# First head pair of a clustered attention kernel: its set-up in a written order, matmuls on zeros instead of warm-up transposes

## The chip, the cores and the metric

The kernel runs on one core of one Trainium2 chip. The metric is the device time of one execution in microseconds (us). The kernel before the change took 858.32 us, the median of three runs (855.65 to 859.44).

## The reference

Three steps. An attention in which a query sees only the keys of its own cluster, then an MLP with SiLU, then a gated MLP.

```python
q_n, k_n, c_n = (normalised q, k, centroids)
q_assign = argmax(einsum('bhsd,hcd->bhsc', q_n, c_n))
k_assign = argmax(einsum('bhsd,hcd->bhsc', k_n, c_n))
mask = q_assign[:, :, :, None] == k_assign[:, :, None, :]
scores = where(mask, scale * q @ k.T, -1e9)
attn = exp(scores - max(scores))
x = (attn / (sum(attn) + 1e-9)) @ v
g = silu(x @ w_in) @ w_out
out = (sigmoid(g @ w_gate) * (g @ w_val)) @ w_out2
```

There are 2 batches, 8 heads, 768 positions, 64 numbers per head and 16 clusters per head. The MLPs work on 1536 tokens of 512 numbers, with hidden sizes 2048 and 1536. All inputs are float32.

## The kernel before, in words

Two heads form a pair, with 64 partitions each, so there are eight pairs. float32 operands are split into a high part, rounded to the matmul's type, and a low part, the rest. For q, the high part is qh and the low part ql; for k, kh and kl.

`load(p)` fetches qq, kk and vv of pair p, 384 KB each (lines 83 to 92). `prep(p)` (line 174) makes a pair ready:

- It casts qh and kh on ACT and subtracts for ql and kl. For pair 0 that is on DVE, for later pairs on POOL. These four buffers are single (pool `st`), so a later pair's casts must wait until everything that reads the earlier pair's has ended.
- Twelve transfers inside the chip, 192 KB each, lay the halves out for the score matmuls (lines 199 to 205), six for each head j: qa holds qh and ql side by side, ka holds kh twice, and the upper or lower half of q2 and k2 (qm, km) holds qh and kl.
- 24 matmuls `pm` multiply the halves with the normalised centroids cc (line 212). DVE sums them into `sim`, and finds the nearest cluster with a maximum, a comparison, a product with `rank`, a second maximum and a last comparison (lines 220 to 243). The result is a one-hot row per position, oh.
- PE transposes oh, and 16 rows per head go into the free half of q2 and k2. For pair 0, ACT and DVE copy them (lines 254 to 264). For later pairs, one ACT copy and four small transfers do it (lines 266 to 273). A score matmul over these rows adds a large negative number wherever the clusters differ.
- ACT and POOL split vv into vs (lines 276 to 279).

Then come the tiles: `scores` (line 288) runs four matmuls into s, DVE takes the row maximum nm, ACT the exponential e. `transposes` turns e into ph and pl on PE, ACT, DVE and POOL. `values` multiplies them with vs. Two tiles of scores run ahead of the rest.

Before pair 0, the centroids are normalised (csq, the r chain, c2), transposed (pc) and split into cc (lines 109 to 140). 13 transposes of the identity run on PE ahead of pc (lines 128 to 130).

The program is written with a framework that reorders instructions by priority and a modelled time, and adds the semaphores. Every engine then runs its own list strictly in order, so an instruction that waits holds up all behind it on that engine. SP issues all DMAs in the order of its list. `issue_after(x)` places DMAs behind the instruction x.

Of the kernel before, what the change touches and what calls it, by code (L numbers as in the profile page):

```python
# [8 lines left out]
F32 = mybir.dt.float32  # L9
# [16 lines left out]
WARM = 13  # L26
# [4 lines left out]
def clustered_attention_then_two_mlps(ctx, tc, qT, kT, v, cen, w1i, w1o, w2g, w2v, w2o, out):  # L31
# [31 lines left out]
    with ExitStack() as att:  # L63
# [29 lines left out]

        cn = cp.tile([P, D], F32, tag="cn", name="cn")
        nc.sync.dma_start(cn, cen)
# [10 lines left out]
        nc.scalar.activation(sq, sq, AF.Sqrt)  # L106

# [15 lines left out]
        nc.vector.reciprocal(r5, r4)  # L123
        c2 = cp.tile([P, 2, D], F32, tag="c2", name="c2")
        nc.vector.tensor_scalar_mul(c2[:, 0, :], cn, r5)
        nc.vector.tensor_scalar_mul(c2[:, 1, :], cn, r5)

        pw = ps_v.tile([P, P], F32, tag="v", name="pw")
        for _ in range(WARM):
            nc.tensor.transpose(pw, ident, ident)  # L130
# [4 lines left out]
        nc.vector.memset(cc.bitcast(F32), 0.0)  # L135
        pcv = pc[:, 0:P].rearrange("p (h j c) -> p h j c", j=2, c=C)
        for j in range(2):
            r = slice(j * D, (j + 1) * D)
            nc.vector.tensor_copy(cc[r, :, j, 0, :], pcv[r, :, j, :])
            nc.vector.tensor_tensor(cc[r, :, j, 1, :], pcv[r, :, j, :], cc[r, :, j, 0, :], op=ALU.subtract)  # L140


        rank = cp.tile([P, 4 * NT, C], BF16, tag="rank", name="rank")
        for c in range(C):
            nc.vector.memset(rank[:, :, c : c + 1], float(C - c))

        rowscale = cp.tile([P, 1], F32, tag="rowscale", name="rowscale")
        nc.vector.memset(rowscale[0:D, :], -MASKED)
        nc.vector.memset(rowscale[D:P, :], 1.0)


        ex = sm.tile([P, 1], F32, tag="ex", name="ex", bufs=1)
        nc.scalar.activation(ex, cc[:, 0, 0, 0, 0:1], AF.Exp)

        q2, k2 = [], []
        for i in range(2):
            for lst, nm in ((q2, "q2"), (k2, "k2")):
                t = cp.tile([P, 2, S], R32, tag=f"{nm}_{i}", name=f"{nm}_{i}")  # L160
                nc.gpsimd.memset(t[D:P, 0].bitcast(F32), 0.0)
                nc.gpsimd.memset(t[0:D, 1].bitcast(F32), 0.0)
                lst.append(t)

        oh = []
        for i in range(2):
            t = cp.tile([P, NT, 4, 32], BF16, tag=f"oh_{i}", name=f"oh_{i}")
            nc.gpsimd.memset(t, 0.0)
            oh.append(t)

        heads = {}
        L, U = slice(0, D), slice(D, P)

        def prep(p):
# [12 lines left out]
            dma = nc.sync.dma_start  # L187

            nc.scalar.activation(qh, qq, AF.Copy, scale=scale)
            if p == 0:  # L190
                nc.vector.scalar_tensor_tensor(ql, qq, scale, qh, op0=ALU.mult, op1=ALU.subtract)
            else:
                nc.gpsimd.tensor_scalar(qq, qq, scale, 1.0, op0=ALU.mult, op1=ALU.mult)
                nc.gpsimd.tensor_tensor(ql, qq, qh, op=ALU.subtract)
            yield
            cast(nc.scalar, kh, kk)
            (nc.vector if p == 0 else nc.gpsimd).tensor_tensor(kl, kk, kh, op=ALU.subtract)
# [9 lines left out]
            for n, (hi, lo) in enumerate(((qh, ql), (kh, kl))):  # L207
                pm = ps_s.tile([P, 512], F32, tag="s", name=f"pm{p}_{n}")
                pv = pm[:, 0 : NT * 4 * C].rearrange("p (t g) -> p t g", t=NT)
                for i in range(NT):  # L210
                    for m, t in enumerate((hi, lo)):
                        nc.tensor.matmul(
                            pv[:, i, :],
                            lhsT=t[:, i * P : (i + 1) * P],
                            rhs=cc[:, p % HP].rearrange("p j a c -> p (j a c)"),
                            start=m == 0,
                            stop=m == 1,
                        )
                yield
                nc.vector.tensor_reduce(  # L220
                    sim[:, n],
                    pm[:, 0 : NT * 4 * C].rearrange("p (t j a c) -> p j t c a", j=2, a=2, c=C),
                    axis=AX.X,
                    op=ALU.add,
                )

            o = oh[p % 2]
            for ns in ((0,), (1,)) if p == 0 else ((0, 1),):
                g, w = 2 * NT * ns[0], 2 * NT * len(ns)
                sg = sim[:, ns[0] : ns[-1] + 1].rearrange("p n j t c -> p (n j t) c")  # L230
                mx = wk.tile([P, w], F32, tag="mx", name=f"mx{p}_{g}")
                nc.vector.tensor_reduce(mx, sg, axis=AX.X, op=ALU.max)
                yield
                eq = wk.tile([P, w, C], BF16, tag="eq", name=f"eq{p}_{g}", bufs=1)
                nc.vector.tensor_tensor(eq, sg, mx.unsqueeze(2).to_broadcast([P, w, C]), op=ALU.is_equal)
                wq = wk.tile([P, w, C], BF16, tag="wq", name=f"wq{p}_{g}", bufs=1)
                nc.vector.tensor_tensor(wq, eq, rank[:, g : g + w], op=ALU.mult)
                yield
# [392 lines left out]
```

## Time and profile before

| | |
|---|---|
| median of three runs | 858.32 us (855.65 to 859.44) |
| the profiled execution, its own time | 857.65 us |
| its span, first to last instruction | 855.6 us |
| PE busy | 812.7 us (95%) |
| DVE, ACT, POOL busy | 544.5, 427.9, 174.5 us |
| DMA, mean over the span | 85 GB/s, 72.46 MB moved |
| first exponential starts | 22.25 us after the span's start |

Times in rows are microseconds from the span's start. In a timeline row, the first number is the start and the second the duration, or, with a count such as x2, the time from the first start to the last end. A bracket at its end gives the engine's idle time before it and what ended that time. "issue" means that the profile names no releaser. In a windows row, each engine has its busy time and its number of instructions; behind POOL stand the granted clock of TensorE, the mean busy share of the 16 DMA engines, and the rate that they moved.

### The profile page before, as it was taken

Reading aid. Unit: us, or ns where it says so; the run is one execution under the profiler, and the core shown is the slowest. Engines: PE = TensorE matmul, PEld = TensorE weight load, DVE = VectorE, ACT = ScalarE, POOL = GpSimd, SP = SyncE. Lnnn points to the kernel's source line nnn. Section 1 sums busy time; section 2 is a strip of 40 time slices with the busy share of each in tenths; the row PEclk is TensorE's granted clock in tenths of the full one; section 3 lists DMA queues with packets and bytes.
Section 4 is the critical chain, followed back from the end, with each engine's and each line's share of the span. In section 5 each row is a group of like instructions: output and inputs, shape, how many; then the busy total and the mean of one; then the engine's idle time right before and its main releaser. Section 6 shows DMA issues by size and latency. Waiting matters only on the chain.

```text
span 855.6 us, 11571 instructions
## 1 busy us (share of the span) xinstructions
PE 812.7 (95%) x4252; PEld 698.9 (82%) x4252; DVE 544.5 (64%) x940; ACT 427.9 (50%) x830; POOL 174.5 (20%) x205
## 2 busy tenths in 40 slices
PE   6898888989989799999999999999999999999998
PEld 5787888978979678888888888888888888888886
DVE  5697697787898886556565556856533656275222
ACT  4686887877969646454154154343334343043200
POOL 5637467466653600000000000000000000000000
PEclk9999999999999999999999999999999999999999
DMA  9552734626540142312212212112111312020012
GB/s 244 145 113 83 177 81 133 171 50 169 122 151 21 47 151 78 113 52 72 74 50 74 71 53 74 53 47 99 50 49 35 115 50 74 25 74 1 0 50 98
DMA packets 25224, 72.46 MB, mean 85 GB/s; under 512 B 4144, under 2 KB 4240, under 8 KB 25168
## 3 DMA queue, kind: packets, MB, share of 16 engines
q1 hardware_dynamic: 25168, 71.73, 28.6%
q8 instruction: 33, 0.54, 0.3%
q14 instruction: 23, 0.19, 0.1%
HBM read 48.27 MB, written 3.19 MB: 60 GB/s over the span
## 4 chain that ended last, share of the span: by engine, by line
PE 75%; DVE 9%; ACT 5%; DMA 5%; issue 3%; SPq 2%; POOL 0%; ACTq 0%; DVEq 0%
PE h L493 15%; PE y L493 15%; PE acc L570 11%; PE ov L493 11%; PE og L493 11%; PE s L290 4%; PE v L339 4%; PE t L320 3%; ACT e L303 2%; DVE nm L298 2%; DVE pl L330 2%; DMA k<-rows 1%; ACT ph L57 1%; DMA kk<-in_kT 1%; DMA qq<-in_qT 1%
## 5 line engine op out<-in xcount | busy, mean ns | idle before, releaser
L57 ACT ACTIVATE wh<-c 128x512 fp32r<-128x512 f32 x68 | 42.8, 632 | 127.6 <-PE y L493 58.9
L320 PE MATMUL t<-ident,e 128*128 128x128 f32 x576 | 89.0, 280 | 9.6 <-DVE pl L330 8.3
L298 DVE TENSOR_REDUCE nm<-s 128x1 f32<-128x768 f32 x96 | 91.1, 949 | 9.1 <-PE s L290 8.2
L330 DVE TENSOR_TENSOR pl<-t,ph 128x384 fp32r<-128x384 f32 x144 | 76.7, 550 | 31.4 <-ACT ph L57 29.2
L303 ACT ACTIVATE e<-s,nm 128x768 f32<-128x768 f32 x96 | 87.0, 907 | 11.6 <-DVE nm L298 10.7
L57 ACT ACTIVATE gh<-g 128x512 fp32r<-128x512 f32 x84 | 53.0, 632 | 76.2 <-DVE g L555 73.7
L505 DVE TENSOR_TENSOR gl<-g,gh 128x512 fp32r<-128x512 f32 x84 | 58.0, 691 | 49.1 <-ACT gh L57 48.8
L339 PE MATMUL v<-ph,vs 128*128 128x256 f32 x288 | 80.7, 307 | 7.3 <-DVE xf L351 5.1
L474 DVE TENSOR_TENSOR wl<-c,wh 128x512 fp32r<-128x512 f32 x68 | 47.7, 705 | 60.5 <-ACT wh L57 60.4
L320 PEld LDWEIGHTS t<-ident,e 128*128 128x128 f32 x576 | 69.2, 143 | 15.7 <-DVE pl L330 10.4
L339 PE MATMUL v<-pl,vs 128*128 128x256 f32 x288 | 79.9, 306 | 1.4 <-DVE pl L330 1.4
L493 PE MATMUL h<-xh,wh 128*128 128x512 f32 x192 | 75.7, 394 | 2.0 <-ACT wh L57 2.0
L493 PE MATMUL h<-xh,wl 128*128 128x512 f32 x192 | 75.4, 393 | 1.3 <-DVE wl L474 1.3
L493 PE MATMUL y<-gh,wh 128*128 128x512 f32 x192 | 74.3, 390 | 1.3 <-issue 1.3
L493 PE MATMUL h<-xl,wh 128*128 128x512 f32 x192 | 75.2, 392 | 0.0
L493 PE MATMUL y<-gh,wl 128*128 128x512 f32 x192 | 74.6, 390 | 0.1
L493 PE MATMUL y<-gl,wh 128*128 128x512 f32 x192 | 74.4, 389 | 0.0
L57 ACT ACTIVATE ph<-t 128x384 fp32r<-128x384 f32 x144 | 67.2, 491 | 13.2 <-PE t L320 12.3
L339 PEld LDWEIGHTS v<-ph,vs 128*128 128x128 f32 x288 | 58.0, 202 | 10.0 <-ACT ph L57 6.1
L290 PE MATMUL s<-ka,qa 128*128 128x384 f32 x192 | 57.3, 381 | 8.5 <-ACT e L303 4.4
L339 PEld LDWEIGHTS v<-pl,vs 128*128 128x128 f32 x288 | 58.2, 202 | 1.6 <-DVE pl L330 1.6
L555 DVE TENSOR_TENSOR g<-ov,g 128x512 f32<-128x512 f32 x36 | 24.9, 692 | 51.8 <-PE ov L493 51.8
(123 smaller groups left out, 1858.9 us busy)
## 6 DMA issues: line engine op xcount, KB each, us to landing
r<-in_w1i SPq DMA_DIRECT2D x16, 512.0 KB, 3.2
r<-in_w1o SPq DMA_DIRECT2D x16, 512.0 KB, 3.2
ka<-kh SPq DMA_DIRECT2D x32, 192.0 KB, 3.9
r<-in_w2g SPq DMA_DIRECT2D x12, 512.0 KB
r<-in_w2v SPq DMA_DIRECT2D x12, 512.0 KB, 3.2
r<-in_w2o SPq DMA_DIRECT2D x12, 512.0 KB, 3.2
qq<-in_qT SPq DMA_DIRECT2D x8, 384.0 KB, 4.8
kk<-in_kT SPq DMA_DIRECT2D x8, 384.0 KB, 3.6
```

The costliest lines, as they stand in the source:

```text
L57: return nc.scalar.activation(o, i, AF.Copy)
L290: nc.tensor.matmul(s[:, g, 0:HS], lhsT=a[:, j, i * P : (i + 1) * P], rhs=c[:, j, g * HS : (g + 1) * HS], start=n == 0, stop=n == 1,)
L298: nc.vector.tensor_reduce(nm, s[:, :, 0:HS], axis=AX.XY, op=ALU.max, negate=True)
L303: nc.scalar.activation(e, s[:, :, 0:HS], AF.Exp, bias=nm, scale=1.0, accum_out=tots[p][:, n : n + 1])
L320: nc.tensor.transpose(t[:, n, :], e[:, kt * P : (kt + 1) * P], ident)
L330: nc.vector.tensor_tensor(lsl, t, hsl, op=ALU.subtract)
L339: nc.tensor.matmul(o, lhsT=vs[:, j, kt, :], rhs=t[:, kt, :], start=kt == 0 and n == 0, stop=kt == NT - 1 and n == 1,)
L474: nc.vector.tensor_tensor(lo, w, hi, op=ALU.subtract)
L493: nc.tensor.matmul(o, lhsT=s[:, k, :], rhs=t[k], start=k == 0 and n == 0, stop=k == KD - 1 and n == 2)
L505: nc.vector.tensor_tensor(gl[k, n], src, gh[k, n], op=ALU.subtract)
L555: nc.vector.tensor_tensor(g, ov, g, op=ALU.mult)
L570: nc.tensor.matmul(o, lhsT=s[k, n][:, sl], rhs=r, start=k == 0 and i == 0, stop=k == KD - 1 and i == 2)
```

## The change

It concerns pair 0 and what is set up before it.

1. Pair 0's preparation leaves `prep` and is written out by hand inside `manual_schedule`, which keeps the written order: the loads cn, qq, kk, the centroids, the casts, the twelve transfers with head 0's six first and vv's load between the two sixes, the clusters and head 0's masks.
2. A mask set now holds q and k of one head (`first_masks(j)`), where it held both heads of q, then of k. Head 0's set is in the written part, head 1's stands in the program behind the first two tiles of scores, as does the split of vv.
3. `load(1)` comes behind the last of the twelve transfers (`issue_after(last.ins)`).
4. The 13 transposes go. In three places, 9, 3 and 10 matmuls of 128x512 on a tile of zeros are issued, the last ten behind pm.
5. Smaller pieces: identb is cast on ACT instead of DVE, cc is built on all 128 partitions in two operations instead of on halves in four (a factor `mine` makes the other head's part zero), `rank` has one row of 16 instead of 24, and the zero fills of q2, k2 and oh are written in another order (`zeros(i)`).

```diff
-WARM = 13
+WARM = (9, 3, 10)
...
+        dma = nc.sync.dma_start
+        first = tc.manual_schedule()
+        first.__enter__()
...
-        load(0)
+        dma(cn, cen)
...
+        dma(qq, qT[0, 0])
+        dma(kk, kT[0, 0])
...
+        wt = cp.tile([P, 512], BF16, tag="wt", name="wt")
+        nc.vector.memset(wt, 0.0)
+        pw = ps_v.tile([P, 512], F32, tag="v", name="pw")
...
+        def warm(n):
+            for _ in range(n):
+                nc.tensor.matmul(pw, lhsT=wt[:, 0:P], rhs=wt, start=True, stop=True)
...
+        warm(WARM[0])
...
-        nc.vector.tensor_copy(identb, ident)
...
+        nc.scalar.activation(identb, ident, AF.Copy)
...
-        for _ in range(WARM):
-            nc.tensor.transpose(pw, ident, ident)
...
+        nc.vector.tensor_copy(cc[:, :, :, 0, :], pcv)
+        nc.vector.tensor_tensor(cc[:, :, :, 1, :], pcv, cc[:, :, :, 0, :], op=ALU.subtract)
+        warm(WARM[1])
...
+        nc.scalar.activation(qh, qq, AF.Copy, scale=scale)
+        nc.vector.scalar_tensor_tensor(ql, qq, scale, qh, op0=ALU.mult, op1=ALU.subtract)
+        cast(nc.scalar, kh, kk)
+        nc.vector.tensor_tensor(kl, kk, kh, op=ALU.subtract)
         for c in range(C):
...
+            nc.vector.memset(rank[:, c : c + 1], float(C - c))
...
+        for j, (r, o) in enumerate(((L, U), (U, L))):
+            dma(qa[r, j].bitcast(F32), qh[r].bitcast(F32))
+            dma(ka[L, j].bitcast(F32), kh[r].bitcast(F32))
+            dma(ka[U, j].bitcast(F32), kh[r].bitcast(F32))
+            dma(qa[o, j].bitcast(F32), ql[r].bitcast(F32))
+            dma(qm[r, j].bitcast(F32), qh[r].bitcast(F32))
+            last = dma(km[r, j].bitcast(F32), kl[r].bitcast(F32))
+            if j == 0:
+                dma(vv, v[0, 0])
...
+        pms = [ps_s.tile([P, 512], F32, tag="s", name=f"pm0_{n}") for n in range(2)]
+        for n, t in enumerate(((qh, ql), (kh, kl))):
+            product_of_clusters(pms[n], 0, t)
+        warm(WARM[2])
...
+        similarities(0, slice(0, 2))
+        similarities(1, slice(0, 1))
+        for _ in first_masks(0):
+            pass
+        first.__exit__(None, None, None)
...
-        for _ in prep(0):
-            pass
         if NPAIR > 1:
-            load(1)
+            with tc.issue_after(last.ins):
+                load(1)
         tiles = [(p, j, i) for p in range(NPAIR) for j in range(2) for i in range(NT)]
         LOOK, LAG = 2, 4
         for t in tiles[:LOOK]:
             scores(*t)
+        zeros(1)
+        for step in (first_masks(1), split_values(vv, vs)):
+            for _ in step:
+                pass
```

The order changes as follows at three places. Names end in numbers: the first is the pair, in s, e and nm the next two are head and tile, in pm, pt, mx, eq, wq and mw the second is a part, and the last number of all is the buffer's.

SP's list, from the first load. Before:

```order
L95 DMA cn_96<-in_cen 128x64
L89 DMA qq0_98<-in_qT 128x768
L90 DMA kk0_99<-in_kT 128x768
L91 DMA vv0_100<-in_v 128x768
L89 DMA qq1_284<-in_qT 128x768
L90 DMA kk1_285<-in_kT 128x768
L91 DMA vv1_286<-in_v 128x768
L200 DMA qa0_192<-qh0_195 64x768
L204 DMA q2_0_176<-qh0_195 64x768
L201 DMA qa0_192<-ql0_196 64x768
```

Now:

```order
L135 DMA qq0_100<-in_qT 128x768
L136 DMA kk0_101<-in_kT 128x768
L232 DMA qa0_173<-qh0_176 64x768
L233 DMA ka0_174<-kh0_178 64x768
L234 DMA ka0_174<-kh0_178 64x768
L235 DMA qa0_173<-ql0_177 64x768
L236 DMA q2_0_127<-qh0_176 64x768
L237 DMA k2_0_129<-kl0_179 64x768
L239 DMA vv0_102<-in_v 128x768
L232 DMA qa0_173<-qh0_176 64x768
```

Head 0's six transfers now stand right behind the first two loads. vv0 comes behind them, and the loads of pair 1 behind all twelve, followed by those of pair 2 as before.

ACT's list, from pair 0's casts to the first exponential. Before:

```order
L57 ACTIVATE kh0_197<-kk0_99 128x768
L57 ACTIVATE vs0_194<-vv0_100 128x6x64 x2
L153 ACT_TABLE_LOAD
L153 ACTIVATE ex_174<-cc_148 128x1
L57 ACTIVATE vs1_336<-vv1_286 128x6x64 x2
L262 ACTIVATE q2_0_176<-pt0_0_262 16x768 x2
L57 ACTIVATE kh1_339<-kk1_285 128x768
L189 ACTIVATE qh1_337<-qq1_284 128x768
L303 ACTIVATE e0_0_0_297,tot0_298<-s0_0_0_290,nm0_0_0_295 128x768
```

Now:

```order
L57 ACTIVATE kh0_178<-kk0_101 128x768
L230 ACT_TABLE_LOAD
L230 ACTIVATE ex_200<-r5_159 128x1
L57 ACTIVATE vs0_175<-vv0_102 128x6x64 x2
L270 ACTIVATE q2_0_127<-pt0_0_264 16x768
L270 ACTIVATE q2_0_127<-pt0_1_315 16x768
L301 ACTIVATE qh1_356<-qq1_275 128x768
L57 ACTIVATE kh1_358<-kk1_276 128x768
L57 ACTIVATE vs1_355<-vv1_277 128x6x64 x2
L370 ACTIVATE e0_0_0_288,tot0_289<-s0_0_0_281,nm0_0_0_286 128x768
```

The casts of pair 1's vv into vs1 stood before pair 0's mask copies, and now stand behind pair 1's other casts and right ahead of the first exponential.

DVE's list, from the end of head 0's mask set to the first row maximum, now:

```order
L256 TENSOR_TENSOR oh_0_131<-wq0_0_258,mw0_0_260 128x6x16 x2
L249 TENSOR_REDUCE sim0_251<-pm0_1_216 128x96
L113 TENSOR_REDUCE mx0_1_305<-sim0_251 128x12
L116 TENSOR_TENSOR eq0_1_307<-sim0_251,mx0_1_305 128x192
L118 TENSOR_TENSOR wq0_1_309<-eq0_1_307,rank_140 128x192
L121 TENSOR_REDUCE mw0_1_311<-wq0_1_309 128x12
L256 TENSOR_TENSOR oh_0_131<-wq0_1_309,mw0_1_311 128x6x16 x2
L271 CAST k2_0_129<-pt0_0_264 16x768
L271 CAST k2_0_129<-pt0_1_315 16x768
L365 TENSOR_REDUCE nm0_0_0_286<-s0_0_0_281 128x1
```

Head 1's whole mask set (mx0_1 to its oh) stands ahead of the copy of head 0's masks into k2. Before, two sets stood there as well, one of q and one of k, with both copies behind them.

## Rows read from the trace of the kernel before

**Rows 1.** The page, parts 1 (busy time of engines) and 4 (chain by engine).

```profile
PE 812.7 (95%) x4252; PEld 698.9 (82%) x4252; DVE 544.5 (64%) x940; ACT 427.9 (50%) x830; POOL 174.5 (20%) x205
...
PE 75%; DVE 9%; ACT 5%; DMA 5%; issue 3%; SPq 2%; POOL 0%; ACTq 0%; DVEq 0%
```

**Rows 2.** Windows of the start: busy by engine, granted clock, DMA share, GB/s.

```profile
2.90:5.20 2.30, 1.47 (x7) 1.47 (x8) 1.82 (x9) 1.10 (x3) 2.14 (x5) 1.00 1.01 375
5.20:12.00 6.80, 5.65 (x28) 5.28 (x26) 3.66 (x10) 3.43 (x6) 5.45 (x7) 1.00 0.99 290
12.00:21.60 9.60, 6.27 (x27) 4.66 (x27) 5.87 (x13) 4.06 (x6) 2.06 (x2) 1.00 1.04 242
...
25.20:34.50 9.30, 9.30 (x74) 9.20 (x72) 5.48 (x9) 5.64 (x13) 4.22 (x5) 1.00 0.88 202
```

**Rows 3.** Timeline, 28 to 37 us: a transfer of pair 1, ACT's longest wait.

```profile
28.55 0.60 SPq L204 DMA_DIRECT2D q<-qh  x1
...
34.56 0.84 ACT L189 ACTIVATE qh<-qq 128x768 fp32r<-128x768 f32 x1 [3.20 <-issue]
```

**Rows 4.** Tile q, the issue at 28.55: time from issue to landing.

```profile
DMA to landing us min/median/max: 5.9/5.9/5.9
```

**Rows 5.** The page, part 6 (DMA issues): count, size of each, time to landing.

```profile
ka<-kh SPq DMA_DIRECT2D x32, 192.0 KB, 3.9
...
qq<-in_qT SPq DMA_DIRECT2D x8, 384.0 KB, 4.8
```

**Rows 6.** Timeline, 0 to 8 us: load, centroids, identity, casts.

```profile
1.18 0.42 SPq L89 DMA_DIRECT2D qq<-in_qT  x1
...
2.60 0.26 ACT L111 ACTIVATE csq<-cn 128x64 f32<-128x64 f32 x1 [0.37 <-DMA cn<-in_cen]
...
3.38 0.29 POOL masks.py:199 TENSOR_SCALAR_AFFINE_SELECT ident<-ident 128x128 f32<-128x128 f32 x1
...
3.73 3.04 PE L130 MATMUL pw<-ident 128*128 128x128 f32 x13 [3.73 <-POOL ident masks.py:199]
...
4.24 0.84 ACT L189 ACTIVATE qh<-qq 128x768 fp32r<-128x768 f32 x1 [1.06 <-DMA qq<-in_qT]
...
4.86 0.35 DVE L126 TENSOR_SCALAR c<-cn,r 128x64 f32<-128x64 f32 x1
...
5.12 0.96 DVE L191 SCALAR_TENSOR_TENSOR ql<-qq,qh 128x768 fp32r<-128x768 f32 x1
...
6.56 0.42 PE L132 MATMUL pc<-ident,c 128*128 128x128 f32 x1
```

**Rows 7.** Timeline, 8 to 23 us: clusters, masks, first scores and exponential.

```profile
8.34 0.40 PE L212 MATMUL pm<-cc,ql 128*128 128x64 f32 x1
...
8.55 0.40 PE L212 MATMUL pm<-cc,qh 128*128 128x64 f32 x1
...
11.84 0.94 ACT L57 ACTIVATE vs<-vv 128x384 fp32r<-128x384 f32 x2 [1.77 <-DMA vv<-in_v]
...
13.57 0.55 DVE L220 TENSOR_REDUCE sim<-pm 128x192 f32<-128x384 f32 x1
...
15.62 0.36 DVE L243 TENSOR_TENSOR oh<-wq,mw 128x192 bf16<-128x192 bf16 x1
...
15.68 0.98 PE L290 MATMUL s<-ka,qa 128*128 128x384 f32 x2 [2.24 <-DVE mw L240]
...
19.19 1.93 DVE L264 CAST k<-pt 16x768 fp32r<-16x768 bf16 x2 [3.22 <-PE pt L254]
...
20.24 1.62 PE L290 MATMUL s<-k,q 128*128 128x384 f32 x4 [1.09 <-issue]
...
22.25 0.90 ACT L303 ACTIVATE e<-s,nm 128x768 f32<-128x768 f32 x1 [0.75 <-DVE nm L298]
```

**Rows 8.** Timeline, 30 to 31 us: two of pair 1's pm matmuls.

```profile
30.49 0.28 PE L212 MATMUL pm<-cc,qh 128*128 128x64 f32 x1
...
30.60 0.28 PE L212 MATMUL pm<-cc,ql 128*128 128x64 f32 x1
```

More of the change, by code (lines that the diff above doesn't have):

```diff
@@ L152, in clustered_attention_then_two_mlps @@
         ex = sm.tile([P, 1], F32, tag="ex", name="ex", bufs=1)
[L153 to L169, printed above, removed]
@@ new lines, in first_masks @@
+        def first_masks(j):
+            sg = sim[:, j].rearrange("p n t c -> p (n t) c")
+            wq, mw = yield from ranked(0, j, sg, 2 * NT)
+            for n in range(2):
+                sl = slice(n * NT, (n + 1) * NT)
+                nc.vector.tensor_tensor(
+                    oh[0][:, :, j, n, 0:C],
+                    wq[:, sl, :],
+                    mw[:, sl].unsqueeze(2).to_broadcast([P, NT, C]),
+                    op=(ALU.not_equal, ALU.is_equal)[n],
+                )
+            pt = ps_t.tile([P, 1024], BF16, tag="t", name=f"pt0_{j}")
+            for i in range(NT):
+                nc.tensor.transpose(
+                    pt[0:D, i * P : (i + 1) * P], oh[0][:, i, j].rearrange("p n c -> p (n c)"), identb
+                )
+            if j == 0:
+                similarities(1, slice(1, 2))
+            r = (slice(D, D + C), slice(0, C))[j]
+            nc.scalar.activation(qm[r, j], pt[0:C, 0:S], AF.Copy, scale=-MASKED)
+            nc.vector.tensor_copy(km[r, j], pt[32 : 32 + C, 0:S])
+            yield
@@ L174, in prep, with split_values @@
+        similarities(0, slice(0, 2))
[3 more added lines that the diff above has]
+        first.__exit__(None, None, None)
+        def split_values(vv, vs):
+            for j in range(2):
+                hi, lo = (vs[:, j, :, L], vs[:, j, :, U]) if j == 0 else (vs[:, j, :, U], vs[:, j, :, L])
+                cast(nc.scalar, hi, vv[:, j])
+                nc.gpsimd.tensor_tensor(lo, vv[:, j], hi, op=ALU.subtract)
+                yield
         def prep(p):
@@ L206, in prep @@
             yield
-            for n, (hi, lo) in enumerate(((qh, ql), (kh, kl))):
+            for n, halves in enumerate(((qh, ql), (kh, kl))):
                 pm = ps_s.tile([P, 512], F32, tag="s", name=f"pm{p}_{n}")
[L209 to L218, printed above, removed]
+                product_of_clusters(pm, p, halves)
                 yield
@@ L274, in prep @@
[L274 to L279 removed]
+            for n in range(2):
+                sl = slice(n * 2 * NT, (n + 1) * 2 * NT)
+                nc.vector.tensor_tensor(
+                    o[:, :, :, n, 0:C].rearrange("p t j c -> p j t c"),
+                    wq[:, sl, :].rearrange("p (j t) c -> p j t c", j=2),
+                    mw[:, sl].rearrange("p (j t) -> p j t", j=2).unsqueeze(3).to_broadcast([P, 2, NT, C]),
+                    op=(ALU.not_equal, ALU.is_equal)[n],
+                )
@@ new lines, in prep @@
+            yield
+            pt = ps_t.tile([P, 1024], BF16, tag="t", name=f"pt{p}")
+            for i in range(NT):
+                nc.tensor.transpose(pt[:, i * P : (i + 1) * P], o[:, i].rearrange("p j n c -> p (j n c)"), identb)
+            rows = wk.tile([P, S], F32, tag="rb", name=f"rows{p}")
+            nc.scalar.activation(rows, pt[:, 0:S], AF.Copy, scale=rowscale)
+            for n, t in enumerate((qm, km)):
+                dma(t[D : D + C, 0].bitcast(F32), rows[32 * n : 32 * n + C])
+                masked[p] = dma(t[0:C, 1].bitcast(F32), rows[64 + 32 * n : 64 + 32 * n + C])
@@ L281, in clustered_attention_then_two_mlps @@
+            yield
+            yield from split_values(vv, vs)
         prob = {}
```

139 lines of the change are left out of this document (65 added, 74 removed).

## The prediction

> **What bounds the kernel now.** I read the page's shares and chain first, then the stages up to 34.5 us, then ACT's longest wait there and the transfer that ends it, then the rows of the start.
>
> Over the whole span PE is the bound: busy 95%, and 75% of the chain that ended last [rows 1]. The change touches only what comes before the first pair runs freely. From the second pair's tiles on, the instructions stand in the same order as before, so whatever the first stage wins or loses goes on to the end one for one, unless something later in that stage waits anyway.
>
> Something does. From 2.9 us the DMA engines are full: shares of 1.01, 0.99 and 1.04, and 0.88 in a last stretch in which the queue runs dry [rows 2]. ACT is idle for 3.20 us, from 31.36, before it casts the third pair's qq into qh at 34.56 [rows 3]. The page names no releaser ("issue"), so I looked for one. The qh buffer is single, so the cast must wait until the second pair's transfers out of it have landed. The last of these is q<-qh, issued at 28.55 and landed 5.9 later [rows 3, 4], at 34.45, 0.11 before the cast. All of ACT's later work stands behind it. I call this **the gate**: PE, DVE and ACT reach it early and wait for the DMA queue.
>
> **The change, part by part, against the gate.** What must land before it is the same in both kernels: nine loads of 384 KB, 23 on-chip transfers of 192 KB (twelve of the first pair, eleven of the second) and the small cn [rows 5]. Only their order and the idle time between them change. I count from the second load's landing; the first is in when qh starts at 4.24 [rows 6]. Prices: 393 kB at 375 GB/s, 1.05 us for a load, and 197 kB at 242 GB/s, 0.81 us for an on-chip transfer [rows 2]. So the second load is in at 5.3.
>
> *The loads' order.* Before, vv0 and the second pair's three loads were queued at once and filled the engines while ACT and DVE made qh, kh, ql and kl. Now the queue runs dry at 5.3. The first transfer needs qh. On ACT the identb cast now stands in front of csq and waits for ident (3.38+0.29=3.67 [rows 6]). Its own 0.3 for 128 columns is an estimate between csq's 0.26 for 64 and qh's 0.84 for 768 [rows 6]. So csq goes from 2.60 to 3.97, and qh from 4.24 to about 4.6, done 5.45. An issue into an empty queue moves data 2.0 later (qq: issued 1.18, in by 4.24, less 1.05 of moving [rows 6]), at 7.45: **2.15 idle**. Three transfers then last to 9.9. The fourth needs ql, which DVE now makes behind cc instead of before it. The scaled centroids were done at 4.86+0.35=5.21, 2.61 after csq began; from 3.97 that is 6.6, so pc stands where it stood, at 6.56. Two cc operations of some 0.35 each (estimated from the c row) and a subtraction of 0.96 [rows 6] behind pc's end at 6.98 give ql at 8.7, and its data at 10.7: **0.8 idle** more. Idle in all: 2.95.
>
> *The gate's new time.* 5.3 + 2.95 + 7 loads x 1.05 + 23 x 0.81 = 34.2 if every transfer has its clean price. Before, the same transfers took from 5.3 to 34.45, 29.15 instead of 26.0; with that duration the gate is at 37.4. The truth lies between, since six loads now stand in one block (clean price) and the on-chip transfers mix as before. I take the middle, 35.8: **+1.35 us**, ends -0.25 and +2.95.
>
> A rule weighed here: the Trainium skill, DMA: Bandwidth & Descriptors, Rules for kernel authors, says to issue a DMA early, compute, and wait late, so that the fixed cost overlaps. It speaks against moving vv0 and the second pair's loads back; by it the sum is +2.95, without it -0.25. The full queue of rows 2 bears it out for the old order.
>
> *Matmuls on zeros for transposes.* The page grants TensorE 1.00 from the start, but the pace says otherwise: pm matmuls start 0.21 apart at 8.34 and 0.11 apart at 30.49 [rows 7, 8]. So the set-up ran at the 1.2 GHz level, after 3.04 us of transposes [rows 6], and later at 2.4. Twenty-two matmuls of 512 columns are added. No row has one at the lower level: four of 384 columns took 1.62 at 20.24 [rows 7], 0.40 each, which bounds one from below; scaled by columns it is 0.54, which bounds it from above, since the 1.62 holds a tail. I take 0.45. Nine (4.1) lie under the loads and are done before pc. Three after pc end near 8.4, and pm began near 8.1 and now waits for ql anyway. Ten stand after pm and *in front of the first scores*: 4.5 at the lower level, half at the upper.
>
> *Masks.* DVE's set for k took 13.57 to 15.98, 2.4 [rows 7]. Now a set holds q and k of one head, but the second head's set still stands on DVE ahead of the first head's k copy, and its transposes on PE ahead of the first mask matmul. So the first exponentials still come two sets, two copies (1.93) and 1.13 (21.12 to 22.25 [rows 7]) after pm's end: 7.9. At the lower level pm ends at 13.6, as before (24 x 0.21 behind 8.5), the ten zeros at 18.1, scores and transposes 3.5 later (15.68 to 19.19) at 21.6, the second copy (0.97) and 1.13 more: 23.7. At the upper, pm's last twelve follow kl (9.7) at 0.11, end at 11.0, and e0 can start at 18.9. The sixteen small memsets of rank move behind kl and lie under pm.
>
> *ACT's order.* e0 now stands behind qh1, kh1 and two vs1 casts (0.94 [rows 7]; they ran at 11.84 before). vv1 lands at 5.3+2.95+12x0.81+4x1.05=22.2, so e0 starts at 23.1 at the earliest, against 22.25, whatever PE's clock. Before, ACT needed 31.36-22.25=9.1 from e0 to the gate; now it arrives at 32.2 to 32.8. The gate is at 35.8, so this loss and any gain on PE are hidden; without that cover the loss would be 0.9 to 1.5. POOL's memsets are the same in number and cost nothing under the loads.
>
> **The sum.** 857.65 (the profiled execution; span 855.6; the median 858.32 is 0.67 higher) + 1.35 = 859.0. Two DVE orders behind the gate differ by an operation; I give them nothing. Half a per cent, 4.3 us, is about what a measurement of this kernel can tell from no change. My forecast is no change.
>
> **Rivals.**
> - *The clock decides, faster.* If zeros lift the clock early and the second pair's loads arrive in time, e0 comes at 18.9, 3.3 earlier, and the four mask matmuls at 20.24 (1.62 [rows 7]) take half, 0.8 less: 853.5. For it: the two paces. Against it: vv1 would have to land at 18, and the gate to come at 30.4, with 26 us of transfers behind 5.3. The Trainium skill, TensorE: Matmul & The Clock Gate, Part 4, says that a transposing matmul does not count as busy for the clock in the same way; by that rule the old warm-up bought nothing and this rival gets its first half. The pace at 8.34 agrees.
> - *The queue starves, slower.* With the bubbles in full, loads at the mixed rate of 290 GB/s (1.36) and transfers at the last stretch's 202 (0.97 [rows 2]), the gate is at 5.3+2.95+9.5+22.3=40.1, 5.6 later: 863.3. It decides once a transfer costs over 0.9. For it: that stretch's rate. Against it: part of that stretch is the queue's own end.
> - *It doesn't do what it says.* The scheduler has put the second head's masks ahead of the first head's scores; if transfers also keep the engines full, both gate and e0 stay: 857.7.
>
> **How the numbers follow.** Forecast 0.62, faster rival 0.13, starved queue 0.13, nothing moved 0.12. The forecast and the last lie within 0.5%: same 0.74. The forecast alone spans 857.4 to 860.6; with half of each outer rival, and the scatter of the three runs (855.65 to 859.44), the range is 854.8 to 862.8.
>
> **What would show it.** Right: a DMA share clearly under 1 between 5.3 and 10.7; ACT's wait before the third pair's qh still there, ended by a landing near 35.8 though PE runs at the faster pace; e0 right behind the vs1 casts at 23 or later. Wrong: no such wait, or a landing by 33 or after 38; e0 before 22; or a difference that appears only behind 60 us, where both orders are equal.

## The result and the profile after

The changed kernel takes 862.31 us, the median of seven runs (861.32 to 866.51); the kernel before, run beside it, 858.32 (855.10 to 860.83). The ratio is 1.0055, 95% interval [1.0028, 1.0082]: slower, by half a per cent. Twelve more runs of the changed kernel gave 1.0038 [1.002, 1.0057]. All 19 have a mean of 862.5, the 42 of the kernel before beside them 859.1: about 3.4 us lost, where the sum had 1.35 and the forecast was no change. The time lies inside the range of the prediction and outside the forecast's own span of 857.4 to 860.6.

The profiled execution took 862.31, its span 860.4. Page, part 1 (busy time of engines) and part 4 (chain by engine), to set against [rows 1]:

```profile
PE 820.5 (95%) x4261; PEld 701.2 (81%) x4261; DVE 545.8 (63%) x943; ACT 427.3 (50%) x831; POOL 174.6 (20%) x205
...
PE 75%; DVE 10%; ACT 5%; DMA 5%; issue 2%; SPq 1%; POOL 1%; POOLq 0%; ACTq 0%; DVEq 0%
```

The bound is the same. Now the start. Windows of the changed kernel, columns as in [rows 2], and then two of the same windows of the kernel before:

```profile
2.90:5.30 2.40, 1.93 (x6) 0.55 (x4) 1.25 (x10) 1.48 (x5) 2.25 (x5) 1.00 0.73 287
5.30:7.50 2.20, 1.06 (x5) 0.49 (x5) 1.61 (x6) 2.17 (x3) 2.20 (x4) 1.00 0.49 113
7.50:10.70 3.20, 2.69 (x13) 2.58 (x14) 1.70 (x18) 0.16 (x1) 1.03 (x2) 0.54 0.94 207
10.70:21.60 10.90, 9.95 (x43) 6.10 (x42) 7.80 (x17) 3.27 (x5) 1.98 (x3) 0.67 1.01 268
```

```profile
2.90:5.30 2.40, 1.57 (x8) 1.57 (x9) 1.92 (x9) 1.13 (x4) 2.24 (x5) 1.00 1.02 376
5.30:7.50 2.20, 1.68 (x8) 1.28 (x6) 2.09 (x5) 0.81 (x1) 2.11 (x4) 1.00 0.88 257
```

The DMA queue, full before, is now short of full by 0.27 x 2.40 + 0.51 x 2.20 + 0.06 x 3.20 = 1.96 us; the kernel before lost 0.26 in the second of these windows. The prediction had 2.95 of idle time.

Timeline of the changed kernel: zeros, pm, the first exponential, and the gate. It answers [rows 3], [rows 6] and [rows 7].

```profile
1.18 3.65 PE L145 MATMUL pw<-wt 128*128 128x512 bf16 x9 [1.18 <-DVE sq L154]
...
6.42 0.81 PE L145 MATMUL pw<-wt 128*128 128x512 bf16 x3
...
8.40 0.40 PE L102 MATMUL pm<-cc,qh 128*128 128x64 f32 x1
8.61 0.40 PE L102 MATMUL pm<-cc,ql 128*128 128x64 f32 x1
...
13.09 4.47 PE L145 MATMUL pw<-wt 128*128 128x512 bf16 x10
...
20.55 0.97 PE L357 MATMUL s<-k,q 128*128 128x384 f32 x4 [0.69 <-DVE k L271]
...
23.36 0.94 ACT L57 ACTIVATE vs<-vv 128x384 fp32r<-128x384 f32 x2 [0.55 <-DMA vv<-in_v]
24.20 0.88 ACT L370 ACTIVATE e<-s,nm 128x768 f32<-128x768 f32 x1
...
29.46 0.46 SPq L313 DMA_DIRECT2D q<-qh  x1
...
36.75 0.84 ACT L301 ACTIVATE qh<-qq 128x768 fp32r<-128x768 f32 x1 [3.77 <-PE pm L102]
```

ACT's wait is still there. Its end, the third pair's qh cast, is what I call the cast below: 36.75 instead of 34.56. The row names pm as releaser, but the second pair's q<-qh lands at 36.60, 0.15 before, and pm had ended long ago. The first exponential stands right behind the vs1 casts, which waited for their load.

The rest of the loss is elsewhere: from the start of the last exponential to the first matmul of the MLP the changed kernel takes 8.14 us, the kernel before 7.54. I call this **the junction**. Timeline there, the kernel before and then the changed one:

```profile
271.26 0.33 SPq L380 DMA_DIRECT2D d_rb<-rt  x1
...
272.62 1.24 SPq L382 DMA_DIRECT2D rb<-d_rb  x2
...
276.63 1.84 POOL L369 TENSOR_TENSOR xf<-xf,rb 128x768 f32<-128x768 f32 x1 [2.62 <-DMA rb<-d_rb]
...
282.34 0.93 ACT L303 ACTIVATE e<-s,nm 128x768 f32<-128x768 f32 x1
...
289.88 0.50 PE L493 MATMUL h<-xh,wh 128*128 128x512 f32 x1 [1.12 <-ACT wh L57]
```

```profile
274.64 0.33 SPq L447 DMA_DIRECT2D d_rb<-rt  x1
...
277.09 1.12 SPq L449 DMA_DIRECT2D rb<-d_rb  x2
...
281.07 1.84 POOL L436 TENSOR_TENSOR xf<-xf,rb 128x768 f32<-128x768 f32 x1 [3.65 <-DMA rb<-d_rb]
...
285.70 0.93 ACT L370 ACTIVATE e<-s,nm 128x768 f32<-128x768 f32 x1
...
293.84 0.50 PE L563 MATMUL h<-xh,wh 128*128 128x512 f32 x1 [1.12 <-ACT wh L57]
```

The seventh pair's row sums go to device memory in a small transfer (d_rb, 6 KB) and come back as rb. SP waits for the first to land before it issues the second: 1.36 between the issues before, 2.45 now, though the order on every engine is the same here (all lists are equal from about 62 us on). POOL starts xf 5.37 after d_rb before, 6.43 now, and behind xf on POOL stand casts that the last `values` on PE wait for. DMA view of the first 1.3 us of this transfer, the kernel before and then the changed one (packets by queue):

```profile
DMA packets 24, 0.01 MB, mean 5 GB/s; under 512 B 12, under 2 KB 24, under 8 KB 24
## 3 DMA queue, kind: packets, MB, share of 16 engines
q1 hardware_dynamic: 24, 0.01, 2.5%
```

```profile
DMA packets 24, 0.03 MB, mean 22 GB/s; under 512 B 11, under 2 KB 22, under 8 KB 22
## 3 DMA queue, kind: packets, MB, share of 16 engines
q8 instruction: 1, 0.02, 5.7%
q14 instruction: 1, 0.01, 2.1%
q1 hardware_dynamic: 22, 0.01, 1.8%
```

The transfer consists of 24 packets. Before, all were through. Now 22 are, and two packets of kind "instruction" have started: program code being fetched. The two are not alike. The one of q8 starts 1.23 behind the issue of d_rb, and the kernel before has one at 1.29, just outside its view, which held nothing. The one of q14 is new at this place: it starts at 1.04 and takes 0.46, where before it started at 5.47. The two packets that are missing from the view move at 1.49 and 1.52, as q14's ends; before, the last moved at 0.95. So the trace points to q14's. The held packets account for 0.57 of the 1.09; the rest of it stays open. What brings such a packet there was a question for the experiments.

### The profile page after: what moved, and what is told of

Its sections match the earlier page's. It is cut to its first block, busy times and chain, and to the rows that moved or that the text cites. A ratio compares the mean times of both kernels' runs of the same rounds, so it can differ in the third digit from the quotient of the medians.

```text
span 860.4 us, 11592 instructions
## 1 busy us (share of the span) xinstructions
PE 820.5 (95%) x4261; PEld 701.2 (81%) x4261; DVE 545.8 (63%) x943; ACT 427.3 (50%) x831; POOL 174.6 (20%) x205
## 4 chain that ended last, share of the span: by engine, by line
PE 75%; DVE 10%; ACT 5%; DMA 5%; issue 2%; SPq 1%; POOL 1%; POOLq 0%; ACTq 0%; DVEq 0%
PE y L563 15%; PE h L563 14%; PE acc L640 11%; PE ov L563 11%; PE og L563 11%; PE v L406 4%; PE s L357 4%; PE t L387 3%; ACT e L370 2%; DVE nm L365 2%; DVE pl L397 2%; ACT ph L57 1%; DMA qq<-in_qT 1%; DMA kk<-in_kT 1%; DVE oh L330 1%
## 5 line engine op out<-in xcount | busy, mean ns | idle before, releaser
L406 PE MATMUL v<-ph,vs 128*128 128x256 f32 x288 | 83.2, 314 | 5.7 <-DVE xf L418 4.1
L406 PE MATMUL v<-pl,vs 128*128 128x256 f32 x288 | 81.7, 311 | 0.0
```

Source lines behind the costliest of these rows:

```text
L406: nc.tensor.matmul(o, lhsT=vs[:, j, kt, :], rhs=t[:, kt, :], start=kt == 0 and n == 0, stop=kt == NT - 1 and n == 1,)
```

## Experiments

All ratios are to the kernel before, run beside on the same chip. "Wait" is the time between the issues of d_rb and rb of the seventh pair.

**The loads' order.** The changed kernel once more, for scatter and for a second profile:

> The changed kernel once more, for a second profile beside the same runs. Queue theory: the first exponential again at 23.5 to 25, the wait before the third pair's qh again ended near 36.6, 861 to 864. Clock theory: if the half-clock stretches fall at other places than in the first profile, the time moves with their number, by up to 1.7 for each; if they fall at the same places, they belong to the program.

Measured: 1.0038 [1.002, 1.0057]; cast 36.20, wait 2.56, junction 8.35.

Loads back in front, in the plainest way:

```diff
+        dma(vv, v[0, 0])
+        load(1)
...
-            if j == 0:
-                dma(vv, v[0, 0])
...
-            with tc.issue_after(last.ins):
-                load(1)
```

> The changed kernel with one part undone: vv0 and the second pair's three loads are issued again right behind the first two, all else as changed (first head's set-up, zeros). Queue theory (the place of the loads costs the time): no idle queue between 5.3 and 7.6 us, ACT's wait before the third pair's qh ends at 34 to 35 instead of 36.6, the first exponential at 21 to 22.5, and the time goes back to 857 to 859.5. Clock theory (the loss is half-clock stretches that the new start brings about at the pair boundaries): time stays at 861 to 864 and the profile has as many half-clock stretches as the changed kernel's. Zeros theory (the ten matmuls in front of the first scores cost it): stays at 861 or more.

Measured: 1.0026 [1.0008, 1.0045], cast 36.50. No clean test: with its data there earlier, the scheduler put vs1 and kh1 in front of the mask copies on ACT, and the first exponential came at 26.38. Only the second pair's loads moved back, in the kernel before (ACT's casts of vs1 and some of POOL's work moved back with them):

```diff
-            load(1)
+            with tc.issue_after(twelve[0].ins):
+                load(1)
```

> The kernel before with one part of the change alone: the second pair's three loads are issued behind the twelve transfers of the first pair (vv0 stays in front). Queue theory: first exponential at 23 to 24.5, the gate 1 to 2.5 later than 34.4, time 860 to 862.5. Clock theory: no change beyond scatter, 857 to 860. Zeros theory: no change, 857 to 860.

Measured: 1.0018 [0.9998, 1.0038], cast 37.72. Against the first profile of the kernel before the gate moved by 3.16; of it 1.0 us (by medians; 1.6 by means) came out at the end, not clear of nothing. So I ran the loads in front with ACT's list held:

```diff
+            with tc.issue_after(copied[0].ins) if p == 1 else nullcontext():
+                nc.scalar.activation(qh, qq, AF.Copy, scale=scale)
```

(and the same for kh1 and vs1; `copied[0]` is the second mask copy).

> The changed kernel with vv0 and the second pair's three loads back in front of the twelve transfers, and ACT's list held as in the changed kernel (the second pair's casts behind the mask copies). Everything else of the change stays. Gate theory (what the change costs is the late loads, through the landing that the third pair's qh cast waits for): that cast is back at 34 to 35.2, from 36.2 and 36.75 in the two profiles of the changed kernel, and the time falls by 1.5 to 2.5, to 860 or below. Theory that the loss lies elsewhere (in what the rest of the change does to the pairs behind): the gate falls as well, and the time stays at 861.5 to 863.

Measured: 1.0028 [1.001, 1.0047], cast 35.25. In this profile the exponentials from the thirteenth to the seventy-ninth start within 1.4 us of the kernel before, on either side (the seventy-ninth 0.11 earlier); the loss comes behind them: 2.3 us in the seventh pair, and a junction of 8.88. The start was undone, and the time only in part.

**The gate, larger and smaller.** Six transfers more in front of it (written to a scratch place, read by nobody):

```diff
+            with tc.issue_after(twelve[0].ins):
+                for n in range(6):
+                    spare = dr.tile([P, S], F32, tag=f"spare{n}", name=f"spare{n}", bufs=1)
+                    nc.sync.dma_start(spare, qT[0, 0])
```

> The kernel before with six more transfers of 384 KB that nobody reads (from the input to a scratch place in device memory), queued behind the first pair's twelve, in front of the third pair's loads and the second pair's transfers. Gate theory, one for one: six times 1.05 to 1.36 put the third pair's qh cast 6.3 to 8.2 later, at 41 to 43, and the time rises by as much, to 864.5 to 867. Theory that the time behind absorbs part of a late gate (as the kernel before with only the second pair's loads moved suggests: cast 3.16 later, median 0.95 higher): a third, 861 to 862.5.

Measured: 1.0068 [1.0043, 1.0093], 5.6 us by medians; cast 40.17, 5.61 later, less than the 6.3 to 8.2 expected. In the time that is one for one, but the scheduler also changed the lists of PE, DVE and ACT up to about 70 us, so the gate is not the only difference. And two transfers less, in the kernel before, where no other engine's list changes:

```diff
+                with tc.issue_after(twelve[0].ins) if p == 2 else nullcontext():
+                    nc.sync.dma_start(kk, kT[b, hp])
+                    loaded[:] = [nc.sync.dma_start(vv, v[b, hp])]
```

> The kernel before with two of the third pair's loads (kk and vv) behind the second pair's twelve transfers instead of in front of them; no other engine's list changes. Gate theory: the third pair's qh cast comes two loads earlier, 2.1 to 2.7, at 31.9 to 32.5, and the time falls by 1 to 2.5. If the first stage is bound by ACT or TensorE as soon as the gate moves forward, or the third pair's kk and vv become late: 0 to 0.5 faster, or slower.

> The kernel before with kk and vv of the third pair behind the second pair's twelve transfers, once more. Gate theory: 1 to 2 under the kernel before, as in the first run (0.998); the cast at 32.5 to 33.5. If the first run was scatter: within 0.5 of it on either side.

Timeline of the first of the two:

```profile
28.12 0.64 SPq L205 DMA_DIRECT2D q<-qh  x1
...
29.79 0.89 SPq L91 DMA_DIRECT2D kk<-in_kT  x1
30.72 0.93 SPq L92 DMA_DIRECT2D vv<-in_v  x1
...
32.64 0.85 ACT L190 ACTIVATE qh<-qq 128x768 fp32r<-128x768 f32 x1 [0.54 <-PE pm L213]
```

Measured: 0.998 [0.9963, 0.9997] and 0.9988 [0.9968, 1.0008]; casts 32.64 and 32.83. The wait of 3.20 has shrunk to 0.54, and both runs come out 1.1 to 1.4 us below the kernel before. The first is the only run whose interval lies below 1. The same edit of the changed kernel:

> The changed kernel with kk and vv of the third pair behind the second pair's twelve transfers; no other engine's list changes. Gate theory: the third pair's qh cast falls from 36.2 to 36.8 to 34 to 35 and the median by 1.3 to 2.2, to 1 to 2 above the kernel before. Theory that the pairs behind lose the time: cast as above, median still 3 above.

Measured: 1.0018 [0.9994, 1.0042], cast 33.70: by the medians about half of the loss is back.

> The version with the loads in front and 13 matmuls on zeros, and with kk and vv of the third pair behind the second pair's twelve transfers. Gate theory: cast at 32.5 to 33.3 and 1 to 2 under the kernel before, about as fast as the kernel before with the same edit (0.998 of it). If ACT is the bound by then (it reaches the cast at 31.4 to 32.8): no more than 0.5 to 1 under.

Measured: 1.0011 [0.9986, 1.0037], cast 34.17, wait 2.42, junction 8.32. No gain: without the two loads moved this version has 0.9994 (below). ACT was idle for only 0.60 ahead of the cast, so the queue hardly holds it any more.

**The gate removed** by a second buffer for qh (`bufs=1 + (t == "qh")`):

> The changed kernel with two buffers for qh instead of one, so that the third pair's cast no longer waits for the second pair's transfers. Gate theory: ACT's wait of 3.5 to 3.9 before that cast goes, and the time falls by 2 or more, to within 1 us of the same edit of the kernel before. Theory that the loss lies elsewhere: the wait goes too, but the time stays 2.5 to 4 above the same edit of the kernel before. If the wait was hidden by later waits in both, neither falls by more than 1.

> The kernel before with two buffers for qh. Gate theory: ACT's wait of 3.20 at 31.36 goes, and 1.5 to 3 of it reach the end: 856 to 857.5. Theory that later waits (on transfers of the second pair, or on the clock's low stretches) take up what the gate gives: 858 to 859.5, no change.

Measured: 1.0038 [1.0018, 1.0057] and 1.0047 [1.0025, 1.0068]. Both expectations of a gain missed. The scheduler moved the cast forward and changed the order behind it as well. In the kernel before the cast now stands ahead of the first exponential and waits 6.46 for the DMA queue, so that the exponential starts at 29.38 instead of 22.25. In the changed kernel the wait is gone and the thirteenth exponential starts at 55.57 (57.61 with one buffer, 55.57 in the kernel before), but the time is no better, with a junction of 8.92 and another order in the pairs. As tests of the gate the two are spoiled by that order; the runs with two loads moved are the clean ones.

**Zeros.**

> The changed kernel without any of the 22 matmuls on zeros (the tile of zeros stays). Queue theory: the zeros lie beside the loads, so the gate stays at 36 to 37 and the time at 861 to 864. Clock theory: TensorE stays at half pace to about 26, the stretches fall elsewhere, time changes by 1 to 3 either way. Zeros theory: 857 to 859.

Measured with `WARM = (0, 0, 0)`: 1.0022 [1.0002, 1.0042], cast 35.49. Its wait is 1.34, but its junction 8.13 (here rb is held: an instruction packet of q8 lies in its time). The interval overlaps those of the changed kernel: the 22 matmuls on zeros gain nothing that shows. (Without them the scheduler also orders the first pair's work otherwise.)

**The fetch of code.**

> The changed kernel with 13 matmuls on zeros (4, 3 and 6) instead of 22, so that TensorE's list has as many matmuls as before; the order behind them stays. Code theory (TensorE's instruction stream is fetched by the same DMA engines in packets, and nine matmuls more have moved a packet onto the two transfers d<-rt and rb<-d of the seventh pair): the wait between these two issues, 2.45 and 2.56 in the profiles of the changed kernel and 1.35 in those of the kernel before, is 1.35 again; the time from the last exponential to the first matmul of the MLP, 8.14 and 8.35, is 7.5 to 7.7; the median is 0.6 to 0.9 under the changed kernel's, so 2 to 3 above the kernel before. Theory that the delay belongs to another part of the change: 2.3 or more, 8.1 to 8.9, no gain. The third pair's qh cast stays at 35.5 to 36.8 by both.

Measured with `WARM = (4, 3, 6)`: 1.0035 [1.0016, 1.0054], cast 35.97, wait 2.57, junction 8.40. Missed: with as many matmuls as before, the delay stays, and the packet of q14 still starts 1.05 behind d_rb. (The order did not stay quite: qh1 and kh1 moved ahead of the second mask copy, and the first exponential came at 26.15.)

> Both suspected costs undone: the loads in front of the twelve transfers with ACT's list held (as in the run before), and 13 matmuls on zeros (3, 0 and 10). If the late gate and the fetch of code are the whole loss: cast of the third pair's qh at 34.5 to 35.3, wait between the two issues of the seventh pair 1.35, last exponential to first MLP matmul 7.5 to 7.7, and the median within 1 of the kernel before. If a third cost is left in the pairs between: 1.5 to 2.5 above it.

Measured, with the loads in front, ACT's list held and `WARM = (3, 0, 10)`: 0.9994 [0.9974, 1.0014], cast 34.89. The loss doesn't show here, though the wait is still 2.40 and the junction 8.30. The same version with two loads moved came at 1.0011 (above), so part of this may be chance.

> The kernel before with nine more small transposes (16 columns) behind the 13, so that TensorE's list has as many matmuls as the changed kernel's; the loads stay as they were. Code theory: the wait between the two issues of the seventh pair rises from 1.35 to 2.3 or more, the time from the last exponential to the first MLP matmul from 7.5 to 8.1 or more, and the median by 0.6 to 0.9. Theory that the delay belongs to another part of the change: 1.35 and 7.5, no change. The third pair's qh cast stays at 34.2 to 34.8.

Measured: 1.0022 [0.9994, 1.0049], wait 2.46, junction 8.54. The delay came as expected, but the nine transposes took 2.13 us and held up pc, and the cast fell to 37.24. So the same with nine matmuls of 16 columns while PE is idle:

```diff
+        for _ in range(9):
+            nc.tensor.matmul(pw[:, 0:16], lhsT=wt[:, 0:P], rhs=wt[:, 0:16], start=True, stop=True)
```

> The kernel before with nine small matmuls on zeros (16 columns) ahead of its 13 transposes, while TensorE has nothing else to do; the order of all else stays. Code theory: the gate stays at 34.2 to 34.8, and the wait between the two issues of the seventh pair rises from 1.35 to 2.3 or more, the time from the last exponential to the MLP from 7.54 to 8.1 or more, the median by 0.5 to 1. Theory that another part of the change makes this delay: 1.35 and 7.5 to 7.6, no change.

Timeline at the junction and DMA view of the transfer's first 1.3 us:

```profile
273.87 0.32 SPq L384 DMA_DIRECT2D d_rb<-rt  x1
...
276.77 1.12 SPq L386 DMA_DIRECT2D rb<-d_rb  x2
...
280.92 1.83 POOL L373 TENSOR_TENSOR xf<-xf,rb 128x768 f32<-128x768 f32 x1 [4.30 <-DMA rb<-d_rb]
...
284.95 0.93 ACT L307 ACTIVATE e<-s,nm 128x768 f32<-128x768 f32 x1
...
293.65 0.50 PE L497 MATMUL h<-xh,wh 128*128 128x512 f32 x1 [1.12 <-ACT wh L57]
```

```profile
DMA packets 23, 0.02 MB, mean 17 GB/s; under 512 B 11, under 2 KB 22, under 8 KB 22
## 3 DMA queue, kind: packets, MB, share of 16 engines
q8 instruction: 1, 0.02, 6.3%
q1 hardware_dynamic: 22, 0.01, 2.3%
```

Measured: cast 34.02, wait 2.90, junction 8.70 instead of 7.54, with nine idle matmuls and the one fill of their tile on DVE as the only edit, 270 us earlier. Again 22 of 24 packets, but beside a packet of q8: it starts 0.35 behind d_rb instead of 1.29 and takes 1.32, and the two late packets move as it ends, at 1.65 and 1.72. So a packet of either queue can hold the transfer, and instructions added at the start can bring it there. In the changed kernel, though, it is q14's that does so. The junction's cost is shown in the trace; in the time, 1.0015 [0.9988, 1.0041], it can't be told from nothing.

> The changed kernel with 20 small matmuls on zeros (16 columns) in front of its first nine; the order of all else stays. Code theory: 40 instructions more move the packet some 4 us ahead of the seventh pair's transfers, the wait between the two issues is 1.35, the time from the last exponential to the MLP 7.5 to 7.7, and the median 0.5 to 1 under the changed kernel's, 2.2 to 3 above the kernel before. Else: 2.3 or more, 8.1 or more, no gain. The gate stays at 36 to 37.

Measured: 1.0055 [1.0028, 1.0081], cast 37.32, wait 2.45, junction 8.21. Missed, and the DMA view of this run says why:

```profile
DMA packets 23, 0.01 MB, mean 10 GB/s; under 512 B 11, under 2 KB 22, under 8 KB 22
## 3 DMA queue, kind: packets, MB, share of 16 engines
q1 hardware_dynamic: 22, 0.01, 1.8%
q14 instruction: 1, 0.01, 1.7%
```

The packet of q8 had moved ahead, as wanted. The one of q14 was still there, and one is enough. The delay isn't due to TensorE's instructions, then: DVE has three more in the changed kernel and ACT one [rows 1]. No run tries which engine q14 serves, but the traces point to DVE. When this packet starts, DVE has begun 448 instructions (waits counted) in all eight profiles with the 940 of the kernel before, and 445 or 446 in ten of the eleven of the changed kernel and its versions, while ACT's count goes from 569 to 593 in the same profiles.

This run also tests the clock rival:

```profile
8.42 0.28 PE L103 MATMUL pm<-cc,ql 128*128 128x64 f32 x1
...
10.65 0.28 PE L103 MATMUL pm<-cc,kl 128*128 128x64 f32 x1
```

Here all pm matmuls run at the faster pace, 0.11 apart, and the last starts at 10.65 instead of 12.88. The first exponential still comes at 24.42, against 24.20.

**Scatter.**

> The kernel before, unchanged. Its median lies within 0.2% of the kernel before run beside it. In its profile the third pair's qh cast starts at 34.2 to 35, the wait between the two issues of the seventh pair is 1.35 and the time from the last exponential to the MLP 7.5 to 7.6; if these differ from the first profile, they are no property of the kernel. The six pairs between take 203.8 in the first profile; 2 more or less would show that their share of the difference is scatter.

Measured: 0.9985 [0.9964, 1.0006]; wait 1.36, junction 7.77; but the cast at 36.10, 1.54 later than in the first profile of the same kernel, with the first exponential at 24.31. The pairs between (thirteenth to eighty-fifth exponential) took 204.3 us, 203.8 in the first profile; over all profiles with one buffer for qh they range from 201.0 to 209.0, the changed kernel's two being 205.1 and 205.7. The expectations above name a clock theory: stretches at the 1.2 GHz level in the pairs. From 40 us to the last exponential the mean granted clock is 0.95 and 0.98 in the two profiles of the changed kernel, with spans of 860.4 and 860.1, and 0.96 and 0.99 in the two of the kernel before, with 855.6 and 858.5. It differs as much between two executions of one kernel, and does not go with the time, so nothing here bears that theory out.

## Why the prediction was wrong

**What held.** The first stage is bound by the queue, and the gate decides: the wait before the third pair's qh cast is there in both kernels, a gate 5.61 later costs 5.6 (with other lists changed too), and one 1.7 to 1.9 earlier than in the first profile gives 1.1 to 1.4 back, with no other list changed. The late loads leave the queue idle between 5.3 and 7.5. e0 stands behind the vs1 casts at 24.20 (I had said 23 or later), so the mask matmuls, now 0.97 instead of 1.62, bring nothing. The rule on early issue, cited from the Trainium skill in the prediction, is borne out at the gate: with the second pair's loads alone moved back, the cast came at 37.72. It has another side: kk and vv of the third pair, moved back behind transfers that were needed sooner, gained.

**The gate's size** was near. With the old loads and order the cast came at 34.56, 34.02 and 36.10 (kernel before twice, and with the small matmuls), with the change's at 36.75, 36.20, 37.32 and 35.97: means of 34.9 and 36.6, 1.7 later, where I had 1.35 (1.5 with the 35.49 of the run without zeros). That it came so near is partly luck, since single profiles of one kernel differ by 1.5, and its parts were off against each other: the idle time is 1.96 instead of 2.95, since DVE had ql done at 8.1 instead of 8.7 and the second bubble hardly exists; and the transfers moved slower than their clean price, about 1.0 us apart instead of 0.81.

**The step that failed** is the sum, which ends at the gate with 1.35 where 3.4 were lost: "whatever the first stage wins or loses goes on to the end one for one, unless something later in that stage waits anyway". I let the change end at the gate, because behind it the instructions stand in the same order, and put all that follows at nothing; a difference that appears only behind 60 us I had named as a sign of being wrong, and there is one. (The lists do differ up to about 62 us, but from the cast to the thirteenth exponential the changed kernel takes 20.86 and 21.33 us, the kernel before 21.01 and 21.57, so that this costs nothing.) From there on the order is the same, but the count of instructions ahead of it is not, and with it the place at which code is fetched. In the changed kernel a fetch falls on a small transfer on which the junction hangs. Junctions: 7.51 to 7.84 in seven profiles of the kernel before and of versions of it without added PE instructions, 8.13 to 8.92 in the eleven of the changed kernel and its versions; 0.6 for the kernel itself (8.14 against 7.54; second profiles 8.35 against 7.77). That a fetched packet holds this transfer is shown by the packets' times in four profiles, and that instructions added at the start can bring it there by the run with nine idle matmuls. Which of the change's instructions moved q14's packet is not shown; the number of matmuls on PE is not the cause, since the delay stays when it is the same as before. The Trainium skill (Runtime: NRT & Kernel Launch, Instruction fetch mechanics) calls the cost of fetching the next block of code mostly hidden; here it is not, in one place: 1.1 us on the transfer, 0.6 at the junction.

**What stays open.** 1.5 to 1.7 at the gate, if it goes on one for one (with only the second pair's loads late, 1.0 to 1.6 of 3.16 did), and 0.6 at the junction are 2.1 to 2.3 of the 3.4. The rest, about 1 us, lies in the pairs between, where single executions of one kernel differ by more than that (204.0 and 202.4 with two loads late); I could not show that it belongs to the change. The traces have a candidate that no run tests. The second pair's row sums take the same way to memory and back, in the kernel before and then the changed one:

```profile
106.10 0.32 SPq L380 DMA_DIRECT2D d_rb<-rt  x1
...
107.44 1.11 SPq L382 DMA_DIRECT2D rb<-d_rb  x2
```

```profile
106.30 0.32 SPq L447 DMA_DIRECT2D d_rb<-rt  x1
...
108.17 1.11 SPq L449 DMA_DIRECT2D rb<-d_rb  x2
```

The issues are 1.34 and 1.87 apart (1.53 and 1.86 in the second profiles), and a packet of q14 starts 0.47 behind the first instead of 4.17. From there to the first exponential of the fourth pair the changed kernel takes 20.23 and 19.88, the kernel before 18.75 and 20.01. It is 19.9 to 21.8 in all eleven profiles of the changed kernel and its versions, and 18.7 to 18.9 in six of the other nine. Whether any of it reaches the end is not shown.

The two versions with the loads in front and ACT's list held differ as well (1.0028 with 22 matmuls on zeros, 0.9994 with 13), and their traces don't tell why. With the loads and nine of the zeros undone the loss no longer shows; which share each has is not settled beyond the gate.

**The clock rival** was wrong for the reason named, that loads set e0: in the run with 20 small matmuls more, pm ran at the faster pace throughout, and e0 came no earlier. Zeros do lift the granted clock, to the 2.4 GHz level from 4.33 on in the first profile (three take 0.81 at 6.42, nine took 3.65), but it was back at 1.2 GHz from 7.74 to 17.98, so that pm ran at 0.21 per matmul as before [rows 7] and the last ten zeros took 4.47. In the second profile of the same kernel it rose at 5.85 and fell at 9.27, and the first pm matmuls started 0.11 apart. It rises behind transposes too: in the kernel before with nine more of them, all pm matmuls start 0.11 apart from 10.05 on, and in the one with six transfers more, behind the usual 13, the first 13 do so from 8.68 on (there too e0 came no earlier, at 22.36). So the sentence on transposes that the prediction cites from the Trainium skill is not borne out by these two profiles; the pace at 8.34 agreed with it in that execution. **The starved queue**, which I gave 863.3, named a price per transfer near the 1.0 us seen, but its gate of 40.1 did not come.

## What to carry to other kernels

Find the transfer that the first stage's longest wait hangs on, and count what is queued in front of it: here two loads that nobody needed yet, put behind it, gave 1.1 to 1.4 us, and were the only edit with a run clearly faster than the kernel before. A small transfer to memory and back with engines waiting on it can be held by code that is fetched on its DMA engines, so a change at the start can cost time at a place that it doesn't touch. Forecast such a change from several profiles if they can be had: one trace gave the gate 1.5 us earlier than another of the same kernel.

## What the runs showed of the hardware

- Code is fetched in packets on the same 16 DMA engines as data (in the changed kernel's page 34 on q8 and 23 on q14, in the kernel before's 33 and 23). One packet beside a 6 KB transfer held two of its 24 packets until it ended: one of 8 KB on q14 in the changed kernel (held to 1.49 and 1.52 instead of 0.95), one of 16 KB on q8 in the run with nine small matmuls (1.65 and 1.72). The time to the next issue grew from 1.36 to 2.45 and 2.90 us.
- A clock lifted early doesn't stay, and the same program gets it at different times. In the first profile of the changed kernel it rose at 4.33, during the first nine matmuls on zeros; PE was idle from 4.83 to 6.29; it fell at 7.74, with pm just begun, and rose again at 17.98, behind the ten zeros that ran from 13.09 to 17.56. In the second it rose at 5.85, fell at 9.27 and rose again at 16.09. It rose behind transposes as well: pm ran at 0.11 per matmul behind 22 of them and, with six transfers more in the queue, behind 13, but at 0.21 behind 13 in both profiles of the kernel before.
- On-chip transfers of 192 KB landed about 1.0 us apart with nothing but themselves in the queue (8.70, 9.57, 10.61, 11.61, 12.68), against the 0.81 that a window with loads and transfers had given.
